# Keys and values of the first and last batch in 1 KB rows, and more transposes of batch 1 by DMA, in an attention-plus-FFN kernel

## The chip, the cores and the metric

The kernel runs on one core of a Trainium2 chip. A core has a matrix engine (TensorE, "PE" in the profile; its weight loads are "PEld"), a vector engine (VectorE, "DVE"), an activation engine (ScalarE, "ACT"), a general engine (GpSimd, "POOL") and a sync engine (SyncE, "SP") that here only issues DMA transfers. The engines run at the same time and wait for one another with semaphores. Matmuls write to PSUM[...]. The metric is the device time of one execution in microseconds (us), the median of several.

## What is computed

```python
# q, k, v: 8 batches, 8 heads, 576 positions, 64 wide, float32
theta = pi / 2 * pos / 576
phi(x) = concat([relu(x) * cos(theta), relu(x) * sin(theta)], axis=-1)   # 64 -> 128
kv  = einsum('bhsf,bhsd->bhfd', phi(k), v);   z = sum(phi(k), axis=s)
num = einsum('bhsf,bhfd->bhsd', phi(q), kv);  den = einsum('bhsf,bhf->bhs', phi(q), z) + 1e-6
x   = num / den                      # as 4608 tokens of 512 (heads side by side)
out = ((x @ w1) * (x @ w2)) @ w3 @ w_out   # 512 -> 1024 -> 1024 -> 512, float32
```

The sum over positions in `kv` does not depend on their order: keys and values may be spread over partitions in any way, as long as both are spread alike and each key row gets the cosine and sine of its own position. Queries are tied to the order of the tokens.

## The kernel before

Each batch's 576 positions are held as five chunks: chunks 0 to 3 with 128 positions (one per partition), chunk 4 with 64. There are two layouts. In the layout of the first and last batch ("own"), partition p holds positions 4p to 4p+3 in chunks 0 to 3, and chunk 4 is a transfer of its own, with rows of one position (64 float32, 256 bytes). In the layout of the other batches the first 64 partitions hold five positions each (rows of 1280 bytes) and the last 64 four each (1 KB):

```python
        at = src[b, :, 0:512, :].rearrange("h (p j) d -> p h j d", j=4)
        eng.dma_start(out=t[rows, :, c0:c0 + n, :].rearrange("p h j d -> p h (j d)"),
                      in_=at[rows, :, c0:c0 + n, :].rearrange("p h j d -> p h (j d)"))

    def load_first4(eng, t, src, b=0):
        eng.dma_start(out=t[0:64, :, 4, :], in_=src[b, :, 512:S, :].rearrange("h p d -> p h d"))

...
    def load(b, which, part=None):
        for name in which:
            src = {"k": k, "v": v, "q": q}[name]
            if part != 1:
                raw[b, name] = raw_tile(name)
            if b in own:
                half = slice(64 * part, 64 * part + 64)
                load_first(nc.gpsimd, raw[b, name], src, b=b, rows=half)
                if part == 1:
                    load_first4(nc.gpsimd, raw[b, name], src, b=b)
                continue
            if part != 1:
                nc.gpsimd.dma_start(
                    out=raw[b, name][0:64, :, :, :].rearrange("p h j d -> p h (j d)"),
                    in_=src[b, :, 0:320, :].rearrange("h (p j) d -> p h (j d)", j=5))
            if part != 0:
                nc.gpsimd.dma_start(
                    out=raw[b, name][64:128, :, 0:4, :].rearrange("p h j d -> p h (j d)"),
                    in_=src[b, :, 320:S, :].rearrange("h (p j) d -> p h (j d)", j=4))
```

Loads from GpSimd turn float32 into bf16 on the way. The keys of batch 0 come as float32 through SyncE. The start of the program:

```python
    k0 = raw[0, "k"] = wst.tile([P, H, NCH, D], FP32, name="kf", bufs=1)
    q0 = raw[0, "q"] = raw_tile("q")
    v0 = raw[0, "v"] = raw_tile("v")
    load_first(nc.sync, k0, k)
    load_first4(nc.sync, k0, k)
    load_first(nc.gpsimd, v0, v)
...
    idle_mms(27)                      # matmuls on zeros, while nothing has landed
    cosv, sinv = _trig_tables(nc, const)   # iotas on GpSimd, the rest on VectorE
    identb = const.tile([P, P], BF16, name="identb")
    load_first4(nc.gpsimd, v0, v)
    load_first(nc.gpsimd, q0, q, 0, 2)
    make_identity(nc, identb[:])
    load_first(nc.gpsimd, q0, q, 2, 2)
    load_w12(0, 256)
    load_w12(256, 256)
    load_first4(nc.gpsimd, q0, q)
    nc.gpsimd.dma_start(out=w1b[:, :, ds(512, 256)], in_=w1v[:, :, ds(512, 256)])

    def other_loads(behind):          # called once x chunk 0 of batch 0 is there
...
        for jp in range(8):
            load_w3(jp)
            if jp == 4:
                load(1, "k")
        load(1, "qv")
```

Features: `phi` of a chunk, its cosine half on VectorE (line 265) and its sine half on ScalarE (line 269). The column `at` of the tables follows the layout. A query chunk is then transposed, by PE and an evacuation of PSUM, or by a DMA transpose that SyncE issues:

```python
    def dma_q(b):
        return order_of(b)[5 if b == 0 else 2 if b == 1 else 0:]   # batch 1's order: 4, 0, 1, 2, 3

    def features(b, dst, src, c, cos=True, sin=True, scalar_heads=H):
        R = ROWS[c]
        at = c if b in own else NCH + c
...                                   # dst[:R, c] <- phi(src[:R, :, c]) with cosv[:R, at], sinv[:R, at]
    def prep_q(b, c):
        features(b, feat_of(b)[1], raw[b, "q"], c)
        if c in dma_q(b):
            R = ROWS[c]
            nc.sync.dma_start_transpose(out=att_of(b)["qpT"][:, :, ds(columns_of(b, c), R)],
                                        in_=feat[b][1][:R, c].rearrange("p h f -> p (h f)"))
```

`num` multiplies a transposed query chunk with `kvs` (the key-value sums) and normalises it into an x chunk; `x_tr` transposes that chunk into `xT`, from which the FFN reads tiles of 512 tokens:

```python
    def num(b, c, chain=True):
...
        def normalize():
            den = sm.tile([P, 2, 4], FP32, name="den")
            nc.vector.tensor_scalar_add(out=den[rows], in0=n4[:, :, :, 64], scalar1=1e-6)
            nc.vector.reciprocal(out=den[rows], in_=den[rows])
            nc.vector.tensor_tensor(out=xblk[rows], in0=n4[:, :, :, 0:D],
                                    in1=den[rows].unsqueeze(3).to_broadcast([R, 2, 4, D]),
                                    op=ALU.mult)

        if chain:
            normalize()
...
    def x_tr(b, c, by_vector=False, pst=None):
...
        if b >= 2:
            nc.sync.dma_start_transpose(out=xT[t][:, :, ds(o, R)], in_=xf)
            return
        if pst is None:
            pst = ps_tr.tile([P, 8, 128], BF16, name="pst")
        for kc in range(4):
            nc.tensor.transpose(pst[:, kc, 0:R], xf[:, ts(kc, 128)], identb[rows, rows])
        copy = nc.vector.tensor_copy if by_vector else nc.scalar.copy
        copy(out=xT[t][:, :, ds(o, R)], in_=pst[:, 0:4, 0:R])
```

The FFN runs tile by tile on PE (w1 and w2 products at line 464, the product with `w34b` at line 510). The other work is put in between by a table of slots: a slot is a place between two groups of FFN matmuls of a tile. Batch 0's first chunks come ahead of tile 0; batch 1 is worked through in slots 6 to 27 of tiles 0 and 1, while PE also multiplies w3 by w_out (line 232):

```python
            spread(prep_units(1, (prep_k,)), 6, 8, between)
            spread(prep_units(1, (prep_q,)), 10, 12, between)
            spread(prep_units(1, (prep_v,)), 13, 13, between)
            attention_at(1, between, kv=(14, 14, 14, 14, 14), tr=(12, 13, 17, 18, 19),
                         nu=(15, 17, 19, 20, 25), xt=(20, 20, 21, 22, 27))
            later = between[24:32]
            for i in range(2):
                between[11 + i].append(lambda i=i: behind_q(1, 2 + 2 * i, 2, "k", i))
            for i, g in enumerate((15, 17, 17, 19)):
                between[g].append(lambda i=i: behind_x(1, (i + 1) // 2, 2, "vvqq"[i], i % 2))
            for jp in range(8):
...                               # w3_tr, w34_mm, between
```

`behind_q(b, i, ...)` and `behind_x(b, i, ...)` make GpSimd wait for a query or x chunk before it issues the load named after it. The start of batch 0, in program order:

```python
    for c in range(NCH):
        prep_k(0, c)
    for c in range(NCH):
        prep_v(0, c)
    kv_steps = kv_first()
    next(kv_steps)
    q0f = feat[0][1]
    features(0, q0f, q0, 0, scalar_heads=4)
    next(kv_steps)
    prep_q(0, 1)
    idle_mms(2)
    q_tr_halves(0, 0)
    prep_q(0, 2)
    idle_mms(1)
    num(0, 0)
    q_tr(0, 1, evac=False)[1]()
    other_loads(att[0]["x"][0][:, 0, 0, 0:1])
    features(0, q0f, q0, 3, sin=False)
    q_tr(0, 2, evac=False)[1]()
    features(0, q0f, q0, 3, cos=False)
    idle_mms(1)
    x_tr(0, 0, by_vector=True,
         pst=unread[:, :].bitcast(BF16).rearrange("p (a b) -> p a b", b=128))
    num(0, 1)
```

Of the kernel before, what the change touches and what calls it, by code (L numbers as in the profile page):

```python
# [19 lines left out]
NCH = 5  # L20
# [48 lines left out]
def kernel(  # L69
# [48 lines left out]
    def raw_tile(name):  # L118
        return ld.tile([P, H, NCH, D], BF16, name=name + "s", bufs=2 if name == "k" else 1)

    def load(b, which, part=None):
        for name in which:
            src = {"k": k, "v": v, "q": q}[name]
            if part != 1:
                raw[b, name] = raw_tile(name)
            if b in own:
                half = slice(64 * part, 64 * part + 64)
                load_first(nc.gpsimd, raw[b, name], src, b=b, rows=half)
                if part == 1:
                    load_first4(nc.gpsimd, raw[b, name], src, b=b)  # L130
                continue
            if part != 1:
                nc.gpsimd.dma_start(
                    out=raw[b, name][0:64, :, :, :].rearrange("p h j d -> p h (j d)"),
                    in_=src[b, :, 0:320, :].rearrange("h (p j) d -> p h (j d)", j=5))
            if part != 0:
                nc.gpsimd.dma_start(
                    out=raw[b, name][64:128, :, 0:4, :].rearrange("p h j d -> p h (j d)"),
                    in_=src[b, :, 320:S, :].rearrange("h (p j) d -> p h (j d)", j=4))

# [13 lines left out]
    v0 = raw[0, "v"] = raw_tile("v")  # L154
    load_first(nc.sync, k0, k)
    load_first4(nc.sync, k0, k)
    load_first(nc.gpsimd, v0, v)
    zeros = const.tile([P, 512], BF16, name="zeros")
# [25 lines left out]

    idle_mms(27)
    cosv, sinv = _trig_tables(nc, const)
    identb = const.tile([P, P], BF16, name="identb")
    load_first4(nc.gpsimd, v0, v)
    load_first(nc.gpsimd, q0, q, 0, 2)
# [11 lines left out]
    def other_loads(behind):  # L201

        seen = sm.tile([P, 1], BF16, name="seen", bufs=1)
        nc.gpsimd.tensor_copy(out=seen[:], in_=behind)
        nc.gpsimd.dma_start(out=w2b[:, :, ds(512, 256)], in_=w2v[:, :, ds(512, 256)])
        load_w12(768, 256)
        nc.gpsimd.dma_start(out=woutb[:], in_=moe_w_out.rearrange("(c p) m -> p c m", p=P))
        for jp in range(8):
            load_w3(jp)
            if jp == 4:  # L210
                load(1, "k")
        load(1, "qv")


# [27 lines left out]
    def dma_q(b):  # L242

        return order_of(b)[5 if b == 0 else 2 if b == 1 else 0:]

# [13 lines left out]

    def features(b, dst, src, c, cos=True, sin=True, scalar_heads=H):  # L260

        R = ROWS[c]
        at = c if b in own else NCH + c
        if cos:
# [11 lines left out]
    def prep_k(b, c):  # L276
        features(b, feat_of(b)[0], raw[b, "k"], c)

    def prep_q(b, c):
        features(b, feat_of(b)[1], raw[b, "q"], c)  # L280
        if c in dma_q(b):
            R = ROWS[c]
            nc.sync.dma_start_transpose(out=att_of(b)["qpT"][:, :, ds(columns_of(b, c), R)],
                                        in_=feat[b][1][:R, c].rearrange("p h f -> p (h f)"))
# [60 lines left out]
    def num(b, c, chain=True):  # L345
# [15 lines left out]
        def normalize():  # L361
            den = sm.tile([P, 2, 4], FP32, name="den")
            nc.vector.tensor_scalar_add(out=den[rows], in0=n4[:, :, :, 64], scalar1=1e-6)  # L363
            nc.vector.reciprocal(out=den[rows], in_=den[rows])
            nc.vector.tensor_tensor(out=xblk[rows], in0=n4[:, :, :, 0:D],  # L365
                                    in1=den[rows].unsqueeze(3).to_broadcast([R, 2, 4, D]),
                                    op=ALU.mult)

# [6 lines left out]
    def x_tr(b, c, by_vector=False, pst=None):  # L375
        R, rows = ROWS[c], out_rows(b, c)
        xblk = att[b]["x"].pop(c)
        xf = xblk[rows].rearrange("p g h d -> p (g h d)")
# [5 lines left out]
        if t not in xT:  # L384
            xT[t] = xtp.tile([P, 4, 512], BF16, name="xT")
        if b >= 2:
            nc.sync.dma_start_transpose(out=xT[t][:, :, ds(o, R)], in_=xf)
            return
        if pst is None:
            pst = ps_tr.tile([P, 8, 128], BF16, name="pst")  # L390
        for kc in range(4):
            nc.tensor.transpose(pst[:, kc, 0:R], xf[:, ts(kc, 128)], identb[rows, rows])  # L392
        copy = nc.vector.tensor_copy if by_vector else nc.scalar.copy
        copy(out=xT[t][:, :, ds(o, R)], in_=pst[:, 0:4, 0:R])  # L394

# [196 lines left out]
    q0f = feat[0][1]  # L592
    features(0, q0f, q0, 0, scalar_heads=4)
    next(kv_steps)
# [7 lines left out]
    other_loads(att[0]["x"][0][:, 0, 0, 0:1])  # L602
    features(0, q0f, q0, 3, sin=False)
    q_tr(0, 2, evac=False)[1]()
    features(0, q0f, q0, 3, cos=False)
    idle_mms(1)
# [15 lines left out]
    for t in range(NT):  # L622
        slots = [[] for _ in range(24)]
        if t == 0:
# [16 lines left out]
            attention_at(1, between, kv=(14, 14, 14, 14, 14), tr=(12, 13, 17, 18, 19),  # L641
                         nu=(15, 17, 19, 20, 25), xt=(20, 20, 21, 22, 27))
            later = between[24:32]
            for i in range(2):
                between[11 + i].append(lambda i=i: behind_q(1, 2 + 2 * i, 2, "k", i))
            for i, g in enumerate((15, 17, 17, 19)):
# [48 lines left out]
```

## Time and profile before

| | |
|---|---|
| time, median of 3 runs | 249.24 us (249.07 to 249.59) |
| span of the profiled execution | 247.4 us |
| granted TensorE clock | 1.000 |
| read from HBM, written | 38.80 MB, 9.44 MB |
| share of 16 DMA engines: loads and stores from GpSimd; SyncE's queue | 72.7%; 33.4% |
| query transposes by DMA, x transposes by DMA | 33, 30 |
| mean time of an x copy out of PSUM, 128x512, ScalarE; VectorE | 0.59 us; 0.42 us |
| first FFN matmul | at 15.85 us |

The profile is of one execution. Its page has the busy time of each engine, the span in 40 slices with the busy share of each in tenths, the DMA queues, and the chain of work that ended last, followed back from the end: at each step to what released the instruction, or to the instruction before it on the same engine. A share of an engine in that chain is time that the result waited for it. Other views are the timeline (start, length, engine, line of the kernel, operation, output<-input, count, and in brackets the idle time before it and what ended it) and the list of waits. Line numbers in views are those of the kernel whose profile it is. Matmuls overlap, so that what one costs is read from the distance of the starts and not from its length. The trace also has the start, size and queue of each DMA packet; a packet is named by the bytes that it reads or writes, and a load that turns float32 into bf16 writes half of what it reads.

### The profile page before, as it was taken

How to read it: one execution, taken by the hardware profiler on the slowest of the kernel's cores; microseconds unless marked ns; L12 is line 12 of the kernel's file. 1: busy time of each engine (PE TensorE's matmuls, PEld its weight loads, DVE VectorE, ACT ScalarE, POOL GpSimd, SP SyncE). 2: the span in 40 equal slices, each digit the busy share in tenths (PEclk: the TensorE clock that was granted, in tenths of full speed). 3: DMA queues.
4: the chain of work that ended last, by engine and by line, in shares of the span. 5: the costliest groups of instructions: out<-in, count | busy, mean ns of one | idle time of the engine just before them, and what ended most of it. 6: DMA issues, size and time to landing. Idle time of an engine off the chain costs nothing.

```text
span 247.4 us, 4896 instructions
## 1 busy us (share of the span) xinstructions
PE 239.9 (97%) x1808; PEld 127.5 (52%) x1839; DVE 141.9 (57%) x333; ACT 123.2 (50%) x209; POOL 94.3 (38%) x189
## 2 busy tenths in 40 slices
PE   8899999999999999999999999999999999999994
PEld 2478555565554445544544455455545554444443
DVE  7776674656657555748465966566586555312421
ACT  2676325927852594267426832783287332323331
POOL 7755241215512442154113621562143008878100
PEclk9999999999999999999999999999999999999999
DMA  6999999999999999999989899999985938999413
GB/s 195 179 193 199 210 204 205 144 160 190 181 119 194 138 154 133 149 158 174 124 134 151 112 153 153 153 181 146 141 108 150 185 82 170 305 300 303 154 41 130
DMA packets 86087, 41.15 MB, mean 166 GB/s; under 512 B 53552, under 2 KB 82608, under 8 KB 86064
## 3 DMA queue, kind: packets, MB, share of 16 engines
q0 software_dynamic: 37072, 27.20, 72.7%
q1 hardware_dynamic: 48560, 13.18, 33.4%
q10 hardware_dynamic: 432, 0.46, 0.5%
q8 instruction: 14, 0.23, 0.4%
q14 instruction: 9, 0.07, 0.1%
HBM read 38.80 MB, written 9.44 MB: 195 GB/s over the span
## 4 chain that ended last, share of the span: by engine, by line
PE 92%; DMA 3%; issue 1%; DVE 1%; POOL 1%; ACT 0%; POOLq 0%
PE ffnps L464 50%; PE ffnps L510 24%; PE ffnps L232 5%; PE pnum L355 4%; PE pnum L297 4%; DMA qs<-in_q_dram 3%; PE pst L220 2%; PE pst L392 1%; PE pst L328 1%; PE ffnps L527 1%; POOL vs L112 0%; DVE xblk L365 0%; PE pfirst L355 0%; ACT xT L394 0%; DVE xT L394 0%
## 5 line engine op out<-in xcount | busy, mean ns | idle before, releaser
L505 DVE TENSOR_TENSOR abT<-asb,ffnps 128x512 bf16<-128x512 bf16 x68 | 46.6, 685 | 56.1 <-PE ffnps L464 55.9
L464 PE MATMUL ffnps<-xT,w1b 128*128 128x512 bf16 (+2 forms) x310 | 74.4, 357 | 0.9 <-ACT xT L394 0.2
L464 PE MATMUL ffnps<-xT,w2b 128*128 128x512 bf16 (+2 forms) x312 | 74.0, 357 | 0.4
L510 PE MATMUL ffnps<-w34b,abT 128*128 128x512 bf16 x271 | 64.7, 379 | 0.4
L501 ACT CAST asb<-ffnps 128x512 bf16<-128x512 f32 x68 | 39.8, 585 | 49.8 <-PE ffnps L464 48.4
L516 ACT COPY held<-ffnps 128x512 f32<-128x512 f32 x35 | 20.5, 586 | 49.6 <-PE ffnps L510 43.6
L464 PEld LDWEIGHTS <-w1b 128*128 128x128 bf16 x320 | 28.9, 98 | 27.7 <-issue 0.6
L464 PEld LDWEIGHTS <-w2b 128*128 128x128 bf16 x320 | 28.7, 98 | 26.9
L510 PEld LDWEIGHTS <-abT 128*128 128x128 bf16 x280 | 25.6, 98 | 26.4
L269 ACT ACTIVATE qp<-qs,sinv 128x512 bf16<-128x512 bf16 (+2 forms) x40 | 28.3, 715 | 2.1 <-DMA qs<-in_q_dram 2.0
L365 DVE TENSOR_TENSOR xblk<-pnum,den 128x512 bf16<-128x512 f32 (+1 forms) x39 | 26.9, 691 | 2.2
L269 ACT ACTIVATE kp<-ks,sinv 128x512 bf16<-128x512 bf16 (+1 forms) x35 | 24.5, 720 | 0.0
L438 POOL DMA_DIRECT2D out_dram<-held x42 | 22.1, 532 | 4.6 <-DMA out_dram<-held 1.8
L540 POOL COPY seen<-xblk 64x1 bf16<-64x1 bf16 x15 | 2.7, 183 | 53.4 <-DVE xblk L365 53.4
L355 PEld LDWEIGHTS <-qpT 128*128 128x128 bf16 x320 | 15.0, 98 | 10.2 <-issue 2.7
L540 POOL COPY seen<-qp 64x1 bf16<-64x1 bf16 x14 | 2.6, 183 | 40.6 <-DVE qp L265 40.6
L265 DVE TENSOR_SCALAR qp<-qs,cosv 128x512 bf16<-128x512 bf16 (+1 forms) x40 | 17.2, 434 | 1.2 <-DMA qs<-in_q_dram 1.2
L363 DVE TENSOR_SCALAR den<-pnum 128x8 f32<-128x8 f32 (+1 forms) x39 | 6.4, 164 | 19.4 <-PE pnum L355 19.4
L289 POOL COPY va<-vs 128x512 bf16<-128x512 bf16 (+1 forms) x30 | 17.5, 632 | 0.0
L297 PEld LDWEIGHTS <-kp 128*128 128x128 bf16 x280 | 13.0, 98 | 7.3
L355 PE MATMUL pnum<-kvs,qpT 128*128 128x65 bf16 x312 | 16.4, 194 | 0.2
L232 PE MATMUL ffnps<-woutb,w3T 128*128 128x512 bf16 x61 | 15.0, 379 | 0.1
(87 smaller groups left out, 184.2 us busy)
## 6 DMA issues: line engine op xcount, KB each, us to landing
out_dram<-held POOLq DMA_DIRECT2D x16, 256.0 KB, 4.6
out_dram<-held POOLq DMA_DIRECT2D x24, 128.0 KB, 3.9
qs<-in_q_dram POOLq DMA_DIRECT2D x10, 256.0 KB, 5.6
w3b<-in_moe_w_dram POOLq DMA_DIRECT2D x8, 256.0 KB, 13.4
ks<-in_k_dram POOLq DMA_DIRECT2D x8, 256.0 KB, 6.0
vs<-in_v_dram POOLq DMA_DIRECT2D x8, 256.0 KB, 6.4
ks<-in_k_dram POOLq DMA_DIRECT2D x6, 320.0 KB, 5.5
qs<-in_q_dram POOLq DMA_DIRECT2D x6, 320.0 KB, 5.3
```

Source lines behind the costliest of these rows:

```text
L232: nc.tensor.matmul(acc[:, :], lhsT=w3T[:, lc, :], rhs=woutb[:, lc, :], start=(lc == 0), stop=(lc == 7))
L269: nc.scalar.activation(out=dst[:R, c, 0:n, D:F], in_=src[:R, 0:n, c, :], func=ACTF.Relu, scale=sinv[:R, at:at + 1], bias=0.0)
L289: eng.tensor_copy(out=feat_of(b)[2][:R, c, :, 0:D], in_=raw[b, "v"][:R, :, c, :])
L297: nc.tensor.matmul(kvt[:, h // 4, ds((h % 4) * 65, 65)], lhsT=kp[:, c, h, :], rhs=va[:, c, h, 0:D + 1], start=(i == 0 and h % 4 == 0), sto ...
L355: nc.tensor.matmul(nt[:, h // 4, ds((h % 4) * 65, 65)], lhsT=qpT[:, h, ds(at, 128)], rhs=kvs[:, h, :], start=True, stop=True)
L365: nc.vector.tensor_tensor(out=xblk[rows], in0=n4[:, :, :, 0:D], in1=den[rows].unsqueeze(3).to_broadcast([R, 2, 4, D]), op=ALU.mult)
L438: eng.dma_start(out=rows[:, :, cols], in_=osb[64 * i:64 * i + rows.shape[0], :, cols])
L464: nc.tensor.matmul(out, lhsT=w[:, kc, ts(jc, 128)], rhs=x[:, kc, tok], start=(kc == 0), stop=(kc == 3))
L501: nc.scalar.copy(out=asb[:], in_=aT[:, :])
L505: nc.vector.tensor_mul(out=abT[:, jc, :], in0=asb[:], in1=bT[:, :])
L510: nc.tensor.matmul(ops[:, :], lhsT=abT[:, jc, ts(ms, 128)], rhs=w34b[:, jc, :], start=(jc == 0), stop=(jc == 7))
L516: nc.scalar.copy(out=osb[:, ms % 2, :], in_=ops[:, :])
```

## The change

Keys and values of batch 0 and of batch 7 take the layout of the other batches, so that no transfer with 256-byte rows is left for them; their queries keep their own. For this `features` is given the column of the tables by its caller. With it, one more query chunk of batch 1 (four of five) and two of its x chunks (3 and 4) are transposed by DMA instead of PE; the first half of batch 2's keys is loaded right behind batch 1's loads, and its second half behind the features of the first query chunk; there are 24 idle matmuls at the start in place of 27; the normalisation of x chunk 0 of batch 0 and the copies of x chunks 0 and 3 are cut in two, so that their steps overlap.

```diff
--- before.py
+++ after.py
@@ -118,25 +118,27 @@
     def raw_tile(name):
         return ld.tile([P, H, NCH, D], BF16, name=name + "s", bufs=2 if name == "k" else 1)
 
+    def load_half(eng, t, src, b, part):
+        if part == 0:
+            eng.dma_start(out=t[0:64, :, :, :].rearrange("p h j d -> p h (j d)"),
+                          in_=src[b, :, 0:320, :].rearrange("h (p j) d -> p h (j d)", j=5))
+        else:
+            eng.dma_start(out=t[64:128, :, 0:4, :].rearrange("p h j d -> p h (j d)"),
+                          in_=src[b, :, 320:S, :].rearrange("h (p j) d -> p h (j d)", j=4))
+
     def load(b, which, part=None):
         for name in which:
             src = {"k": k, "v": v, "q": q}[name]
             if part != 1:
                 raw[b, name] = raw_tile(name)
-            if b in own:
-                half = slice(64 * part, 64 * part + 64)
-                load_first(nc.gpsimd, raw[b, name], src, b=b, rows=half)
-                if part == 1:
-                    load_first4(nc.gpsimd, raw[b, name], src, b=b)
-                continue
-            if part != 1:
-                nc.gpsimd.dma_start(
-                    out=raw[b, name][0:64, :, :, :].rearrange("p h j d -> p h (j d)"),
-                    in_=src[b, :, 0:320, :].rearrange("h (p j) d -> p h (j d)", j=5))
-            if part != 0:
-                nc.gpsimd.dma_start(
-                    out=raw[b, name][64:128, :, 0:4, :].rearrange("p h j d -> p h (j d)"),
-                    in_=src[b, :, 320:S, :].rearrange("h (p j) d -> p h (j d)", j=4))
+            for i in (0, 1) if part is None else (part,):
+                if name == "q" and b in own:
+                    half = slice(64 * i, 64 * i + 64)
+                    load_first(nc.gpsimd, raw[b, name], src, b=b, rows=half)
+                    if i == 1:
+                        load_first4(nc.gpsimd, raw[b, name], src, b=b)
+                else:
+                    load_half(nc.gpsimd, raw[b, name], src, b, i)
 
     woutb = wst.tile([P, 8, DM], BF16, name="woutb", bufs=1)
     w3b = wst.tile([P, 8, DFF], BF16, name="w3b", bufs=1)
@@ -152,9 +154,9 @@
     k0 = raw[0, "k"] = wst.tile([P, H, NCH, D], FP32, name="kf", bufs=1)
     q0 = raw[0, "q"] = raw_tile("q")
     v0 = raw[0, "v"] = raw_tile("v")
-    load_first(nc.sync, k0, k)
-    load_first4(nc.sync, k0, k)
-    load_first(nc.gpsimd, v0, v)
+    for half in range(2):
+        load_half(nc.sync, k0, k, 0, half)
+    load_half(nc.gpsimd, v0, v, 0, 0)
     zeros = const.tile([P, 512], BF16, name="zeros")
     nc.vector.memset(zeros[:], 0.0)
     va_bufs, kp_bufs, qp_bufs = [], [], []
@@ -182,10 +184,10 @@
         for _ in range(n):
             nc.tensor.matmul(unread[:, :], lhsT=zeros[:, 0:128], rhs=zeros[:], start=True, stop=True)
 
-    idle_mms(27)
+    idle_mms(24)
     cosv, sinv = _trig_tables(nc, const)
     identb = const.tile([P, P], BF16, name="identb")
-    load_first4(nc.gpsimd, v0, v)
+    load_half(nc.gpsimd, v0, v, 0, 1)
     load_first(nc.gpsimd, q0, q, 0, 2)
     make_identity(nc, identb[:])
     load_first(nc.gpsimd, q0, q, 2, 2)
@@ -210,6 +212,7 @@
             if jp == 4:
                 load(1, "k")
         load(1, "qv")
+        load(2, "k", 0)
 
 
     w3Ts = {}
@@ -241,7 +244,7 @@
 
     def dma_q(b):
 
-        return order_of(b)[5 if b == 0 else 2 if b == 1 else 0:]
+        return order_of(b)[5 if b == 0 else 1 if b == 1 else 0:]
 
     feat = {}
 
@@ -257,10 +260,9 @@
             att[b] = {"qpT": phi.tile([P, H, S], BF16, name="qpT"), "x": {}}
         return att[b]
 
-    def features(b, dst, src, c, cos=True, sin=True, scalar_heads=H):
+    def features(dst, src, c, at, cos=True, sin=True, scalar_heads=H):
 
         R = ROWS[c]
-        at = c if b in own else NCH + c
         if cos:
             nc.vector.tensor_scalar(out=dst[:R, c, :, 0:D], in0=src[:R, :, c, :], scalar1=0.0,
                                     scalar2=cosv[:R, at:at + 1], op0=ALU.max, op1=ALU.mult)
@@ -274,10 +276,10 @@
                                         op0=ALU.max, op1=ALU.mult)
 
     def prep_k(b, c):
-        features(b, feat_of(b)[0], raw[b, "k"], c)
+        features(feat_of(b)[0], raw[b, "k"], c, NCH + c)
 
     def prep_q(b, c):
-        features(b, feat_of(b)[1], raw[b, "q"], c)
+        features(feat_of(b)[1], raw[b, "q"], c, c if b in own else NCH + c)
         if c in dma_q(b):
             R = ROWS[c]
             nc.sync.dma_start_transpose(out=att_of(b)["qpT"][:, :, ds(columns_of(b, c), R)],
@@ -362,9 +364,12 @@
             den = sm.tile([P, 2, 4], FP32, name="den")
             nc.vector.tensor_scalar_add(out=den[rows], in0=n4[:, :, :, 64], scalar1=1e-6)
             nc.vector.reciprocal(out=den[rows], in_=den[rows])
-            nc.vector.tensor_tensor(out=xblk[rows], in0=n4[:, :, :, 0:D],
-                                    in1=den[rows].unsqueeze(3).to_broadcast([R, 2, 4, D]),
-                                    op=ALU.mult)
+            n = 1 if b == 0 and c == 0 else 2
+            for i in range(2 // n):
+                g = ts(i, n)
+                nc.vector.tensor_tensor(out=xblk[rows, g], in0=n4[:, g, :, 0:D],
+                                        in1=den[rows, g].unsqueeze(3).to_broadcast([R, n, 4, D]),
+                                        op=ALU.mult)
 
         if chain:
             normalize()
@@ -374,7 +379,7 @@
 
     def x_tr(b, c, by_vector=False, pst=None):
         R, rows = ROWS[c], out_rows(b, c)
-        xblk = att[b]["x"].pop(c)
+        xblk = att[b]["x"][c]
         xf = xblk[rows].rearrange("p g h d -> p (g h d)")
         if b % 2 == 0:
             slot = S * b + 128 * c
@@ -383,15 +388,19 @@
         t, o = divmod(slot, 512)
         if t not in xT:
             xT[t] = xtp.tile([P, 4, 512], BF16, name="xT")
-        if b >= 2:
+        if b >= 2 or b == 1 and c >= 3:
             nc.sync.dma_start_transpose(out=xT[t][:, :, ds(o, R)], in_=xf)
             return
         if pst is None:
             pst = ps_tr.tile([P, 8, 128], BF16, name="pst")
-        for kc in range(4):
-            nc.tensor.transpose(pst[:, kc, 0:R], xf[:, ts(kc, 128)], identb[rows, rows])
-        copy = nc.vector.tensor_copy if by_vector else nc.scalar.copy
-        copy(out=xT[t][:, :, ds(o, R)], in_=pst[:, 0:4, 0:R])
+        copies = [nc.vector.tensor_copy if by_vector else nc.scalar.copy] * 2
+        if b == 0 and c == 3:
+            copies[1] = nc.vector.tensor_copy
+        n = 2 if b == 0 and c in (0, 3) else 4
+        for i in range(4 // n):
+            for kc in range(n * i, n * i + n):
+                nc.tensor.transpose(pst[:, kc, 0:R], xf[:, ts(kc, 128)], identb[rows, rows])
+            copies[i](out=xT[t][:, ts(i, n), ds(o, R)], in_=pst[:, ts(i, n), 0:R])
 
     def attention_at(b, slots, kv, tr, nu, xt):
 
@@ -590,7 +599,7 @@
     kv_steps = kv_first()
     next(kv_steps)
     q0f = feat[0][1]
-    features(0, q0f, q0, 0, scalar_heads=4)
+    features(q0f, q0, 0, 0, scalar_heads=4)
     next(kv_steps)
     prep_q(0, 1)
     idle_mms(2)
@@ -600,9 +609,9 @@
     num(0, 0)
     q_tr(0, 1, evac=False)[1]()
     other_loads(att[0]["x"][0][:, 0, 0, 0:1])
-    features(0, q0f, q0, 3, sin=False)
+    features(q0f, q0, 3, 3, sin=False)
     q_tr(0, 2, evac=False)[1]()
-    features(0, q0f, q0, 3, cos=False)
+    features(q0f, q0, 3, 3, cos=False)
     idle_mms(1)
     x_tr(0, 0, by_vector=True,
          pst=unread[:, :].bitcast(BF16).rearrange("p (a b) -> p a b", b=128))
@@ -639,10 +648,9 @@
             spread(prep_units(1, (prep_q,)), 10, 12, between)
             spread(prep_units(1, (prep_v,)), 13, 13, between)
             attention_at(1, between, kv=(14, 14, 14, 14, 14), tr=(12, 13, 17, 18, 19),
-                         nu=(15, 17, 19, 20, 25), xt=(20, 20, 21, 22, 27))
+                         nu=(15, 17, 19, 20, 25), xt=(15, 20, 21, 22, 25))
             later = between[24:32]
-            for i in range(2):
-                between[11 + i].append(lambda i=i: behind_q(1, 2 + 2 * i, 2, "k", i))
+            between[10].append(lambda: behind_q(1, 0, 2, "k", 1))
             for i, g in enumerate((15, 17, 17, 19)):
                 between[g].append(lambda i=i: behind_x(1, (i + 1) // 2, 2, "vvqq"[i], i % 2))
             for jp in range(8):
```

## The prediction

> **What bounds the kernel now.** I read the page first: busy shares, the row of slices, the chain that ended last.
>
> ```profile
> PE 239.9 (97%) x1808; PEld 127.5 (52%) x1839; DVE 141.9 (57%) x333; ACT 123.2 (50%) x209; POOL 94.3 (38%) x189
> ...
> PE   8899999999999999999999999999999999999994
> ...
> PE 92%; DMA 3%; issue 1%; DVE 1%; POOL 1%; ACT 0%; POOLq 0%
> ```
>
> TensorE (PE) works in every slice, and 92% of the chain is matmuls. The rest sits at the front: one DMA wait of 3%. So there are two ways to gain: let the stream of real matmuls begin earlier, or take work out of it. What VectorE, ScalarE and GpSimd save counts only if one of those two follows. The chain over the first 26 us (start, length, what) shows what sets the beginning:
>
> ```profile
> 1.28 1.04 POOL vs L112
> ...
> 3.56 8.02 DMA qs<-in_q_dram
> ...
> 12.60 0.44 DVE qpT L342
> ...
> 14.19 0.70 DVE xblk L365
> ...
> 14.93 0.41 PE unread L392 x4
> ...
> 15.37 0.44 DVE xT L394
> ...
> 15.85 1.05 PE ffnps L464 x16
> ...
> 21.85 0.59 ACT xT L394
> ```
>
> The first FFN matmul runs at 15.85 us. It waits for x chunk 0 of batch 0, that for the first query chunk, which lands at 11.58 (3.56 + 8.02). The keys and values are only just ahead of the query, as the timeline shows (start, length, engine, line, operation):
>
> ```profile
> 6.84 3.17 ACT L269 ACTIVATE kp<-kf,sinv 128x512 bf16<-128x512 f32 x5 [4.61 <-DMA kf<-in_k_dram]
> 9.68 1.25 DVE L289 COPY va<-vs 128x512 bf16<-128x512 bf16 x5 [0.59 <-DMA vs<-in_v_dram]
> 10.03 0.29 PE L314 MATMUL kva<-va,kp 128*128 128x65 bf16 x4 [0.59 <-ACT kp L269]
> ```
>
> Values land at 9.68, their copies run to 10.93, and the key-value matmuls keep pace from 10.03 to about 11.4. From 15.85 on PE hardly waits; the largest wait, some 0.2 us before 22.49, is for the ScalarE copy of x chunk 3 (21.85). Last, I read the PE timeline around batch 1 for the price of the transposes:
>
> ```profile
> 49.17 0.61 PE L328 MATMUL pst<-identb,qp 128*128 128x128 bf16 x8
> 49.61 1.03 PE L232 MATMUL ffnps<-woutb,w3T 128*128 128x512 bf16 x4
> ...
> 57.88 0.62 PE L392 MATMUL pst<-identb,xblk 64*128 64x64 bf16 x8
> 58.40 0.42 PE L355 MATMUL pnum<-kvs,qpT 128*128 128x65 bf16 x8
> ...
> 65.47 0.40 PE L392 MATMUL pst<-identb,xblk 128*128 128x128 bf16 x4
> 65.71 1.03 PE L464 MATMUL ffnps<-xT,w1b 128*128 128x512 bf16 x3
> ```
>
> Because matmuls are pipelined, the price is from one start to the next: 0.44 us for the eight of a query chunk, 0.24 for the four of x chunk 3, and 0.52 for those of x chunks 4 and 0 together, so about 0.28 for chunk 4.
>
> [...] counted by their starts, the packets of values that read 1 KB go at 97 per 0.25 us (397 GB/s read), those that read 256 bytes at 137 (140 GB/s). [...] keys run alone to about 5 us, and values, issued at 1.28, have no packet before 5.5. [...] the weight loads of the idle matmuls are 0.43 us apart until 5.4, and the last fifteen take 3.12 us (0.21 each). So three idle matmuls fewer end the warm-up at about 8.8 instead of 9.44[...].
>
> **The change part by part.** *Start.* Keys and values of batch 0 lose a set of 512 packets of 256 bytes each; the bytes move into 512 rows of 1280 and 512 of 1024. By the rates above, 512 small packets of values take 512/137 x 0.25 = 0.93 us; the same 131 KB at 395 GB/s take 0.33. Saving 0.6. For keys the small packets go at up to 157 per 0.25 us: 0.82 us, against 0.34 at the 385 GB/s of their large ones. Saving 0.48. Both sets lie ahead of the first query packets, and the DMA engines are never idle there, so the query should land about 1.05 us earlier, near 10.5. Before, the main part of a tensor landed without its small rows; now chunks 0 to 3 need both halves. Keys: first part at 6.75 before, all of it 0.3 later now, near 7.05. Values: they begin after the keys; 0.48 saved on keys, 0.33 more bytes of their own to wait for, so 9.4 to 9.5 instead of 9.68. GpSimd also issues half as many descriptors in the first values load (an issue of 512 rows takes 0.70 us at lines 133 and 137, against 1.04), which puts the later issues 0.35 earlier; I count nothing for it, since the data are what is late.
>
> Then the chain: ScalarE's key features end 0.3 later, near 10.3, still ahead of the fifth chunk's matmuls; key-value matmuls end near 11.1 (before about 11.4); the query features start when VectorE is through with the value copies, 10.65, instead of 11.6; PE comes to the query transposes near 11.45 instead of 12.16, after the two idle matmuls that stand there. The start therefore moves by 0.7, not by 1.05: the value copies and key-value matmuls take over as the last wait. Splitting the first normalisation and the first x copy in two lets half 0 be transposed while half 1 is multiplied. Little comes of it, as VectorE is busy with a query feature (0.34) in between: 0.1. Sum at the start: 0.8.
>
> *Chunk 3 of batch 0.* Its x copy is split over ScalarE and VectorE, which takes most of the wait at 22.1 to 22.5: 0.2.
>
> *Batch 1.* One query chunk and two x chunks go from PE to DMA transposes: 0.44 + 0.28 + 0.24 = 0.96 out of the stream. One VectorE copy of 0.42 and two ScalarE copies (0.4 and 0.59) go too, which is off the path.
>
> *Loads after it.* The first half of batch 2's keys is issued without a gate; its second half is gated earlier. It is behind batch 1's values in the same queue, and takes data traffic out of the time in which the query transposes run.
>
> *Last batch.* Two sets of 256-byte rows fewer near 180 us, where PE is full and loads have slack: 0.
>
> What gives some back: batch 1's values are DMA-bound. Their copies begin at 48.84 and end at 50.24, and PE uses them at 50.48. They move by the 1.05 us of DMA saved plus the 0.2 of slack; PE would come 0.8 + 0.2 + 0.44 = 1.44 earlier. Stall 0.2. Sum: 0.8 + 0.2 + 0.96 - 0.2 = 1.76; I take 1.65, since the split copies and the transposes' landing are the less certain terms. 249.24 - 1.65 = 247.6 us.
>
> **The rivals.** *Transposes that land late.* Before, the three query transposes of batch 1, issued at 48.16, 49.6 and 52.25, land 6.3 to 8.0 us later (packets from 51.0 to 57.9), and the chunks are used at 56.67, 58.40 and 63.42. With four of them, an x chunk behind them and the use 1.3 us earlier, the second or third could come 0.5 to 1.5 late, and x chunk 4 (wanted at about 60.1, when tile 1 starts) as well. For it: one issue keeps SyncE's queue 1.3 to 2.5 us. Against it: the first issue moves from 48.16 to about 46.5, because the chunk that was done on PE now leads, and batch 2's keys, which ran in the midst of the transposes at 52 to 54, are mostly gone by then. It would make 248.3 to 249.3. *The start does not move*, because values land no earlier or keys' features become the bound: only the 1.0 to 1.2 of batch 1 and chunk 3 is left, 248.2. *The start moves by the whole 1.05 and Pool's 0.35 as well*: that three idle matmuls (0.65 us) were taken out fits values that come clearly earlier. It would be 247.0. *PE cools down in the longer gap*: [...] I see nothing for it.
>
> **Range and chances.** Everything the change can reach is in the first 66 us and within 2.2 us of gain. 247.6 is the middle; the good rival gives 246.8 with the stall gone, the bad one 248.8. Two per cent are 5 us, three times the gain, so "within 2%" is nearly certain; a stall of 5 us would need a transfer that nothing here points to.
>
> **What would show it.** Right: the query lands near 10.5 and the first FFN matmul comes near 15.05; values near 9.5, keys near 7.05; no PE transposes but one query chunk in batch 1; the FFN of tile 1 at about 60.0 instead of 61.70; from there to the end the same distance as now. Wrong: a wait of PE on a transposed query or on x between 50 and 62; a first FFN matmul after 15.5; key-value matmuls at half clock.

## The result, and the profile after

The changed kernel takes 255.5 us (254.7 to 255.84) against 249.23 before: a ratio of 1.0245, interval 1.0219 to 1.0271, or 6.1 us more by that ratio. The prediction was 247.6 us with a range of 246.8 to 248.8. The span of the profiled execution is 253.9 us against 247.4.

The page of the changed kernel, the lines that answer to those shown of before, and the row of the granted clock:

```profile
PE 240.3 (95%) x1789; PEld 127.7 (50%) x1820; DVE 140.7 (55%) x335; ACT 122.1 (48%) x207; POOL 92.4 (36%) x186
...
PE   8488999998999999999999999999999999999994
...
PEclk9979999999999999999999999999999999999998
...
PE 83%; DMA 10%; DVE 3%; issue 1%; ACT 1%; SPq 0%; DVEq 0%
```

PE is busy for as long as before. The span has grown by time in which PE waits: the second and third slices (6 to 19 us) have a hole, and the clock falls in the third (by the trace it is halved from 13.6 to 17.0 us). DMA is now 10% of the chain instead of 3%. Of that, 9.2 us are the keys at the start. Another 17.3 us are two query transposes under way (6.8 us from 51.40, 10.5 from 172.71); PE does other work during most of them and waits 1.5 us for them in all. The chain over the first 26 us (start, length, what):

```profile
0.74 0.75 SPq L123
...
1.54 9.21 DMA kf<-in_k_dram
...
13.30 0.29 PE kva L316 x4
...
18.45 0.76 DVE xblk L370 x2
...
19.72 0.28 PE unread L402 x2
20.01 0.02 issue
20.03 0.29 DVE xT L403
```

The wait for the query (8.02 us before) has given way to one for the keys: `kf` is complete at 10.75 us, where its main part was there at 6.75. The timeline shows what follows from it:

```profile
10.86 2.20 DVE L267 TENSOR_SCALAR kp<-kf,cosv 128x512 bf16<-128x512 f32 x5 [4.85 <-DMA kf<-in_k_dram]
10.87 3.17 ACT L271 ACTIVATE kp<-kf,sinv 128x512 bf16<-128x512 f32 x5 [8.63 <-DMA kf<-in_k_dram]
...
12.98 1.08 DVE L291 COPY va<-vs 128x512 bf16<-128x512 bf16 x5
...
13.30 0.29 PE L316 MATMUL kva<-va,kp 128*128 128x65 bf16 x4 [4.00 <-DVE va L291]
...
20.38 0.38 PE L473 MATMUL ffnps<-xT,w1b 128*128 128x128 bf16 x4
```

The first FFN matmul runs at 20.38 us instead of 15.85, 4.53 later. The values are no longer what is waited for: their copies (12.98) stand in VectorE's queue behind the key features. The list of PE's waits shows the rest:

```profile
PE kva L316 <- DVE va L291: 4.0, 1, 4.0
PE pnum L357 <- DMA qpT<-qp: 1.5, 2, 1.1
...
PE unread L402 <- DVE xT L403: 0.5, 1, 0.5
PE pst L402 <- ACT xT L403: 0.5, 1, 0.5
```

1.1 us is the first DMA-transposed query of batch 1 (at 58.25), 0.4 a query of batch 7 (at 183.29); the two waits of 0.5 stand in the middle of the split x copies. Laying the ScalarE copies of FFN products of both traces side by side gives the lag of the changed kernel along the way: 4.84 us in tile 0, 5.8 after the first queries of batch 1, 5.26 in tile 1, 5.6 at 110 us, 6.2 near 180, and 6.5 in the span. So 1.2 us of it arise behind tile 1. Each profile is of one execution, and some tenths of such a lag can be chance: in e12 below, which changes only loads of the last batch, it is 0.30 in tile 0 and 0.66 from tile 1 on.

### The profile page after: what moved, and what is told of

The parts are those of the page before. It is cut to its first block, busy times and chain, and to the rows that moved or that the text cites. A ratio compares the mean times of both kernels' runs of the same rounds, so it can differ in the third digit from the quotient of the medians.

```text
span 253.9 us, 4864 instructions
## 1 busy us (share of the span) xinstructions
PE 240.3 (95%) x1789; PEld 127.7 (50%) x1820; DVE 140.7 (55%) x335; ACT 122.1 (48%) x207; POOL 92.4 (36%) x186
## 4 chain that ended last, share of the span: by engine, by line
PE 83%; DMA 10%; DVE 3%; issue 1%; ACT 1%; SPq 0%; DVEq 0%
PE ffnps L473 47%; PE ffnps L519 21%; DMA qpT<-qp 7%; PE pnum L357 4%; PE ffnps L235 4%; DMA kf<-in_k_dram 4%; PE pnum L299 3%; PE pst L223 1%; DVE xblk L370 1%; DVE kp L267 1%; PE ffnps L536 1%; PE pst L402 1%; ACT kp L271 1%; PE kva L316 0%; PE pnum L316 0%
## 5 line engine op out<-in xcount | busy, mean ns | idle before, releaser
L525 ACT COPY held<-ffnps 128x512 f32<-128x512 f32 x35 | 20.5, 586 | 51.7 <-PE ffnps L519 48.5
L291 POOL COPY va<-vs 128x512 bf16<-128x512 bf16 (+1 forms) x30 | 17.5, 632 | 0.2 <-DMA vs<-in_v_dram 0.2
```

Of the source, the lines that this page charges most:

```text
L525: nc.scalar.copy(out=osb[:, ms % 2, :], in_=ops[:, :])
```

## Experiments

The theory after this reading: three parts of the change cost time, each by itself. The largest is the load of the float32 keys in two halves of 64 partitions. First, each part alone, on top of the kernel before; then the mechanism of the two larger ones. Ratios are to the kernel before, run on the same chip.

**e1, the start alone.**

```diff
-    load_first(nc.sync, k0, k)
-    load_first4(nc.sync, k0, k)
-    load_first(nc.gpsimd, v0, v)
+    for half in range(2):
+        load_half(nc.sync, k0, k, 0, half)
+    load_half(nc.gpsimd, v0, v, 0, 0)
...
-    idle_mms(27)
+    idle_mms(24)
...
-    load_first4(nc.gpsimd, v0, v)
+    load_half(nc.gpsimd, v0, v, 0, 1)
```

> The kernel before with the new key and value loads of batch 0 and 24 idle matmuls, nothing else. Theory A ([...] the first half of the float32 keys runs at 205 GB/s and its second half shares the engines with the values): keys land near 10.8 as in the changed kernel, the first FFN matmul comes near 20.2, time 253.5 to 254.2, a ratio of 1.017 to 1.020. Rival B (the late keys are a chance of that one profile, or come from the other changes): keys near 7.1, time 248.5 to 249.

253.93 us, ratio 1.0177 (1.0160 to 1.0194): +4.4 us. Keys land at 10.76, the first FFN matmul runs at 20.33. Theory A; from the timeline:

```profile
10.86 2.20 DVE L266 TENSOR_SCALAR kp<-kf,cosv 128x512 bf16<-128x512 f32 x5 [4.87 <-DMA kf<-in_k_dram]
...
20.33 0.38 PE L470 MATMUL ffnps<-xT,w1b 128*128 128x128 bf16 x4 [0.15 <-DVE xT L400]
```

**e2, batch 1 alone** (`dma_q` from the second chunk on, x chunks 3 and 4 by DMA, `load(2, "k", 0)` without a gate, `behind_q(1, 0, 2, "k", 1)` in slot 10).

> The kernel before with the changes of batch 1 alone: four query chunks and x chunks 3 and 4 by DMA transposes, first half of batch 2's keys ungated. Theory A (these transposes land late by their own doing: four in a row, each taking SyncE 1.3 to 3 us): PE waits about 1.1 to 1.3 us for the first transposed query, which eats the 0.96 us of PE work taken out: 249.2 to 249.9. Rival B (they were late only because everything was late): no wait over 0.2 us, 248.2 to 248.6.

250.18 us, ratio 1.0038 (1.0023 to 1.0053): +0.9 us, above both ranges, though on the side of A. The wait is there with a start that is not late; from the PE timeline:

```profile
53.52 0.43 PE L357 MATMUL pnum<-kvs,qpT 128*128 128x65 bf16 x8 [1.13 <-DMA qpT<-qp]
...
59.23 0.42 PE L357 MATMUL pnum<-kvs,qpT 128*128 128x65 bf16 x8 [0.23 <-DVE xblk L370]
...
62.52 1.03 PE L471 MATMUL ffnps<-xT,w1b 128*128 128x512 bf16 x4
```

Tile 1 begins at 62.52, 0.8 later than before, although PE has less to do. The second wait, 0.23 for a normalisation, is one that the x transposes on PE used to cover. Further on in tile 1 the lag of this profile is 0.53 us; it rises to 1.10 at 110.31, where PE has a wait of 0.41 that ends with key features of ScalarE (`kp`). The changed kernel has such a wait of 0.18 at 114.80. In e4, which has the same changes of batch 1, the lag stays at 0.99 from 87 us to the end, so these later waits may be chance. Nor is the 1.1 us the same in every execution (e4).

**e3, the splits alone** (the `n` and `copies` lines of `normalize` and `x_tr`).

> The kernel before with the split normalisation and the split x copies of chunks 0 and 3 alone. Theory A (the second half's transposes wait for the first half's copy, since both halves are in one PSUM tile: 0.5 us twice in the changed kernel): the first FFN matmul at 16.1 to 16.3 instead of 15.85 and a wait of 0.5 at chunk 3: 249.5 to 250.0. Rival B (the halves overlap as meant): 248.9 to 249.2.

249.85 us, ratio 1.0015 (1.0005 to 1.0025): +0.4 us. Theory A; the timeline around the first copy:

```profile
14.74 0.28 PE L401 MATMUL unread<-identb,xblk 128*128 128x128 bf16 x2
...
15.20 0.28 DVE L402 COPY xT<-unread 128x256 bf16<-128x256 bf16 x1
...
15.53 0.27 PE L401 MATMUL unread<-identb,xblk 128*128 128x128 bf16 x2 [0.50 <-DVE xT L402]
...
16.19 0.38 PE L472 MATMUL ffnps<-xT,w1b 128*128 128x128 bf16 x4
```

The second pair of transposes has its data at 15.02 (both normalisations, 14.26 + 0.76) and starts at 15.53, when the copy of the first pair has ended. Both pairs write one PSUM tile, and the wait ends with the copy that reads that tile (VectorE reads PSUM here, as `xT<-unread` shows); so the program orders the write behind the read. (Halves in two tiles were not tried.) Two halves in sequence take longer than one whole: FFN at 16.19 instead of 15.85. At chunk 3 the same wait is 0.46.

**e4, all but the start** (the changed kernel with the removed lines of e1 put back).

> The changed kernel with batch 0's keys and values as before and 27 idle matmuls. If the parts add up, it is e2 plus e3 minus the time before, plus the loads of the last batch, which should be 0 to 0.4 (one wait of 0.41 for a query of batch 7 in the changed kernel): 249.3 to 250.5 by theory A of both. If the start is the whole of the loss (rival): 247.9 to 248.3.

251.17 us, ratio 1.0074 (1.0053 to 1.0095). The time is above both ranges. The ratios of e2, e3 and e12 (below, 0.0009) add up to 0.0062, which is inside the interval. With e1 the four parts make 0.0239 of the 0.0245: within the intervals the parts add, and no loss from their meeting is measured. The profile of this run shows how much the late query varies: with the same changes of batch 1 as in e2, and batch 2's keys again issued next to the first transpose (47.65 and 47.66), PE waits only 0.24 us for it (at 53.67), and the lag behind the kernel before shrinks by 0.4 us from 32 to 69 us; 0.30 of that is lost again at 75.03, for a query of batch 2. The ten times of this run go from 249.96 to 253.78. So the 1.1 us of e2 and of the changed kernel is what two profiles show and no constant of the change.

**e5, both halves of the keys at once.**

```diff
-    for half in range(2):
-        load_half(nc.sync, k0, k, 0, half)
+    for half, eng in enumerate((nc.sync, nc.scalar)):
+        load_half(eng, k0, k, 0, half)
```

> e1 (the new loads of batch 0 alone) with the two halves of the keys issued at once, one by SyncE and one by ScalarE. Theory A ([...] the two streams do not take from each other): about 380 GB/s together, last key packet near 5.8, keys land near 6.8, values as in e1 or sooner, time 248.4 to 249.4. Rival B (two transfers share the DMA engines and only take turns): as slow together as one after the other, keys near 9 to 10.8, 252.5 to 254.

253.79 us, ratio 1.0163 (1.0130 to 1.0197): rival B. The keys are complete at 9.97:

```profile
9.97 2.06 DVE L266 TENSOR_SCALAR kp<-kf,cosv 128x512 bf16<-128x512 f32 x5 [3.98 <-DMA kf<-in_k_dram]
```

Both halves are issued at 0.7 us. By the packets of the trace ScalarE's half ran alone until 4.46, with 86 to 90 packets of 1 KB per 0.25 us from 3.25 to 3.75 and with 46 to 48 (190 to 197 GB/s) after 4.0. SyncE's had its first packet then and its last at 8.5 (36 to 41 of 1280 bytes per 0.25 us from 6 to 7.75, 184 to 210 GB/s). From 4.5 to 5.25 both were under way, and together moved 186 to 193 GB/s. Why they went almost one after the other, and were no faster while both ran, is not shown.

**e6, PE kept busy** (`idle_mms(46)` in e1).

> e1 with 46 idle matmuls instead of 24, so that PE works until about 12.7 us and keeps its clock. Theory A (of the 4.5 us of late start about 1 is the halved clock in 10 to 17.5 us): granted clock 1.0 throughout, key-value matmuls 0.13 us a group of four instead of 0.22, first FFN matmul at 19.2 to 19.6 instead of 20.33, time 252.8 to 253.3. Rival B (the start follows the landing of the query and keys only): no change, 253.8 to 254.

Busy times and granted clock by stretch (us; then PE, PEld, DVE, ACT, POOL busy, clock, DMA share, GB/s), first of e1:

```profile
12.50:15.00 2.50, 1.69 (x32) 1.69 (x32) 2.28 (x10) 1.94 (x4) 0.33 (x1) 0.50 1.57 192
15.00:17.50 2.50, 2.50 (x24) 1.69 (x22) 0.52 (x2) 1.88 (x4) 0.00 (x0) 0.50 1.45 195
```

and of e6:

```profile
12.50:15.00 2.50, 2.50 (x48) 1.82 (x46) 2.24 (x9) 1.82 (x4) 0.29 (x1) 1.00 1.59 191
15.00:17.50 2.50, 2.39 (x37) 1.70 (x34) 1.50 (x6) 1.99 (x5) 0.00 (x0) 1.00 1.45 196
```

The clock stays whole, and the first FFN matmul runs at 19.04 instead of 20.33, as theory A has it or better. The time does not follow, and is that of B: 253.94 us, ratio 1.0176 (1.0139 to 1.0213), against 1.0177 (1.0160 to 1.0194) of e1. By these intervals a gain of up to about 1 us could be hidden (an estimate: 0.004 of 249 us), a whole 1.3 hardly. In the two profiles the span is 251.6 against 252.1, so 0.8 of the 1.3 us is given back on the way; all of it goes near 160 us, where PE waits 0.66 us for a ScalarE copy in e6 and not in e1. Whether that wait is chance is not known. The halved clock is a cost in the trace that is not found in the time, and this is left open.

**e7, the values after the keys** (e1 with the values' loads behind a GpSimd copy that waits for the second half of the keys).

> e1 with the values issued only when all keys have landed, so that the keys have the DMA engines to themselves. Its time says nothing (later values, 254 to 258); its packets do. Theory A ([...] whatever the row): the second half's 1 KB rows run alone at about 200 GB/s (50 packets per 0.25 us, 85 to 110 ns each) and end near 8.2. Rival B (rows of 1280 bytes are the slow ones): they run at 93 to 96 packets per 0.25 us, 46 ns each, as the 1 KB rows over 128 partitions did, and end near 6.9. Rival C (only the sharing with the values was slow): both halves near 380 GB/s, all keys out by 5.5.

The 1 KB rows of the second half, alone on the engines, ran at 51 to 54 packets per 0.25 us (209 to 221 GB/s), 82 to 88 ns each, from 6.25 to 7.25, and ended at 7.9. Theory A: it is not the length of the row. Nor is sharing with the values the only trouble: without any sharing the keys still take from 2.25 to 7.9. But each half starts faster than it goes on: the first has 75 packets per 0.25 us at 3.5 (384 GB/s) and 37 to 43 from 4.25 to 4.75, the second 61 and 71 from 5.75 to 6.25. Its time, 256.95 us in one run, is that of values that start late.

**e9, the five-position half across partition 64** (e7 with the first half in partitions 32 to 95, the second in 0 to 31 and 96 to 127, its values unmoved: the sums are then of mismatched positions; 255.19 us in one run).

> e7 (keys alone on the engines, values after them) with the five-position half of the keys put into partitions 32 to 95 in place of 0 to 63, and the four-position half into partitions 0 to 31 and then 96 to 127. The value rows stay where they were, so keys and values no longer match: the key-value sums are those of mismatched positions, and the time says nothing. What counts is the key packets. Theory A ([...]): the 1280-byte packets now run at 70 to 80 per 0.25 us (350 to 400 GB/s), 55 to 60 ns each, done by about 4.8; the two pieces of 32 partitions after them at 45 to 52 per 0.25 us (200 GB/s) each. Rival B (any transfer to 64 partitions is slow): 36 to 43 per 0.25 us and 110 to 120 ns, as in e7.

The packets of the keys in the four cases, counted in the traces by their start; this is no view of the profile:

```
keys (float32)                  partitions   window       packets  mean    written
before, 1 KB rows               0-127        4.00-4.25      95     47 ns   389 GB/s
changed, 1280-byte rows         0-63         3.50-3.75      78     55 ns   399 GB/s
changed, 1280-byte rows         0-63         4.50-4.75      35    119 ns   179 GB/s
changed, 1280-byte rows         0-63         5.00-5.25      39    119 ns   200 GB/s
e7, 1 KB rows alone             64-127       6.50-6.75      53     83 ns   217 GB/s
e9, 1280-byte rows              32-95        4.00-4.25      76     55 ns   389 GB/s
```

The same rows, the same 64 partitions in number, and once the load is under way twice the rate, only because the range crosses partition 64. Theory A for these packets, the last of which starts at 5.15, against 5.5 in e7 and 5.8 in the changed kernel. The half rate is no fixed speed of such a load, though: from 3.25 to 4.0 us the changed kernel's went at 292 to 399 GB/s (the second line has the middle of it), and only from 4.0 at 179 to 205. Why the first packets go faster is not shown. For the two pieces of 32 partitions the theory had 45 to 52 packets per 0.25 us; they began with 64 to 92 and then went at 52 to 70. (The last packet of each kind started at 5.7 before, for the 1 KB rows, and at 5.8 and 9.6 in the changed kernel for the first and the second half.)

Once a load into 64 partitions on one side of partition 64 is under way the runs agree: 179 to 221 GB/s. Near its start they do not: up to 399. Why such a load falls to that rate, and one across partition 64 does not, is not shown by these runs. Two queues at once brought nothing: e5 has 253.79 us against 253.93 of e1. Side by side two loads did run at 7.0 us in the changed kernel: keys to partitions 64 to 127 at 164 GB/s written and values to 0 to 63 at 92, together 256, more than either half took alone for long.

**e8, half of batch 2's keys later** (e2 with its second half behind x chunk 4).

> e2 (batch 1's changes alone) with the second half of batch 2's keys issued only behind x chunk 4 of batch 1. Theory A (the first query transposes are held up by the load that runs beside them): packets of the first transpose start 1.2 to 2 us after its issue, no wait of PE for a query over 0.2 us, 248.5 to 249.3 if the late keys cost nothing later. Rival B (a DMA transpose needs its 6 to 7 us here anyway): the wait of about 1.1 us stays, 250 or more.

250.26 us, ratio 1.0022 (1.0008 to 1.0037), which is not clear of e2's 1.0038. The wait for the first query is gone; the PE timeline:

```profile
52.24 0.42 PE L357 MATMUL pnum<-kvs,qpT 128*128 128x65 bf16 x8
...
57.94 0.42 PE L357 MATMUL pnum<-kvs,qpT 128*128 128x65 bf16 x8 [0.23 <-DVE xblk L370]
```

The first transpose, issued at 46.93, has its first packets at 48.5, 1.6 us later, where in e2 they started 2.7 us after the issue at 46.83 and ran among the keys' until 52. So A holds for the wait, and B for the total: the key half now comes too late for ScalarE. The chain of this run:

```profile
54.39 4.75 DMA ks<-in_k_dram
59.23 0.72 ACT kp L271
...
62.05 1.89 PE ffnps L471 x8
```

On ScalarE the late key features (0.72 us from 59.23, 0.62 from 60.42) stand ahead of x copies, the last of which runs from 61.51 to 62.01, and tile 1 begins at 62.05.

**e10, only x chunks 3 and 4 by DMA** (with the x slots of the changed kernel).

> The kernel before with only x chunks 3 and 4 of batch 1 by DMA transposes (query chunks as before). Theory A (x transposes land with slack: chunk 4 is there long before tile 1 wants it): 0.52 us of PE work out of the stream and no new wait, 248.6 to 248.9. Rival B (num of the third chunk then waits 0.23 us for the second's normalisation, as in e2, and the next transposes come later): 249.0 to 249.3.

249.33 us, ratio 0.9991 (0.9978 to 1.0004): closest to B, no difference that is measured. The PE timeline shows the 0.28 of chunk 4 turned into a wait:

```profile
57.85 0.39 PE L392 MATMUL pst<-identb,xblk 128*128 128x128 bf16 x4
58.46 0.42 PE L355 MATMUL pnum<-kvs,qpT 128*128 128x65 bf16 x8 [0.23 <-DVE xblk L365]
```

With eight transposes in that place PE came to `num` when the normalisation before it had ended (58.40 in the kernel before); with four it comes earlier and waits until 58.46. Only the 0.24 of chunk 3 is left, seen as a lead of 0.25 at 66.6 us.

**e11, e2 with batch 2's keys gated as before.**

> e2 (batch 1's changes alone) with both halves of batch 2's keys gated as in the kernel before. Theory A (the wait of 1.1 us for the first transposed query comes from the load that runs beside it; gated later, it starts only after the first transpose has been issued): the wait shrinks to 0 to 0.5, 248.3 to 249.0. Rival B (with the second half gated behind the third and fifth query chunk the loads fall into the same time and the wait stays): 249.8 to 250.3.

252.51 us, ratio 1.0111 (1.0086 to 1.0137): both theories missed, it is worse. The PE timeline:

```profile
53.58 0.43 PE L356 MATMUL pnum<-kvs,qpT 128*128 128x65 bf16 x8 [1.57 <-DMA qpT<-qp]
...
59.40 0.43 PE L356 MATMUL pnum<-kvs,qpT 128*128 128x65 bf16 x8 [1.68 <-DMA qpT<-qp]
```

The load that was issued between the transposes ran ahead of the later ones: from 50.5 to 52 the trace has 424 packets of keys and 18 of transposes. Moving batch 2's keys forward was right, then: by the ratios of e11 and e2 (1.0111 and 1.0038) it saved some 1.8 us of what four transposes would otherwise have cost here. (Both halves move between the two runs.)

**e12, the last batch alone** (batch 7's keys and values in the new rows).

> The kernel before with the new key and value loads of the last batch alone. Theory A: no effect, PE is full there, 249.0 to 249.7 (ratio 0.998 to 1.002). Rival B (the wait of 0.41 us for a query of batch 7 in the changed kernel comes from these loads): 249.7 to 250.0 and such a wait near 177 to 183 us.

249.43 us, ratio 1.0009 (0.9995 to 1.0022). Theory A: no effect that is measured. The longest wait for a transposed query is 0.18, at 57.32, so the 0.41 at batch 7 in the changed kernel does not come from these loads alone.

## Why the prediction was wrong

*What bounds the kernel* was read rightly: a PE stream without gaps behind a front that waits for transfers. Four parts make 0.0239 of the 0.0245, and each of them is in the prediction. "From there to the end the same distance as now" failed in the profile, whose lag grows by 1.2 us behind tile 1, with PE waits of 0.18 and 0.41 there; as e4 has no such growth, this may be chance.

*The start* is the step that failed: "Saving 0.48" for the keys, and with it "keys ... near 7.05" and "the start therefore moves by 0.7". I gave the moved bytes the rate of the large packets seen, 385 GB/s. That rate was measured on rows to all 128 partitions. The new halves go to 64 partitions each and run at about 200: in e7, where nothing else is moving, the keys need 2.25 to 7.9 us, 5.6 us, where 1.18 MB at 385 GB/s would be 3.1 us (an estimate from that rate). The kernel before could not show it: its loads of 64 partitions turn float32 into bf16, and write half of what they read. At 35.5 us it has 150 packets of 640 bytes in half a microsecond, 192 GB/s written and 384 read: such a load reads at nearly the full rate while it writes at that of the halves here. Only the float32 keys, which have the same row length on both sides, would have to write faster. Then the second half, still unsent when the values begin, shares with them (40 packets of keys beside 36 of values per 0.25 us at 7.0 us), which is why they end later in the changed kernel than in e7. So of the 3.7 us by which the keys miss 7.05, 1.7 are the sharing (9.6 against 7.9) and the rest comes with the half rate. Measured: +4.4 us (e1) where -0.7 was predicted, without the splits.

*The values' share*, 0.33 more bytes against 0.93 of small packets, was never reached as a bound: the keys hid it. Whether it would save 0.6 was not tried alone, since keys and values must have one layout.

*The splits*: "0.1" and "0.2" gained, +0.4 measured (e3). I counted what VectorE does in between, and not that the two halves share a PSUM tile, where the second write waited 0.5 us for the first read.

*Batch 1*: the price list of 0.96 us holds as work: from the first 512-wide FFN product to the key-value matmuls of batch 1 the distance is 24.91 us instead of 25.36, the 0.44 of one query chunk. But 0.28 of the rest became a wait for the normalisation (e10), and the query landed late. The rival "transposes that land late" named it with 0.5 to 1.5 us; 1.1 was seen in two profiles (0.24 in e4's), and for the first transposed chunk and not for "the second or third". I had put it aside because batch 2's keys would be "mostly gone by then". They were not: their second half was issued together with the first transpose (46.61 and 46.83 in e2). The part was to gain 0.76 (0.96 less a stall of 0.2) and lost 0.9 (e2): the term is off by 1.7 us. How much of that the late query makes on average is open, since the wait varies.

*The last batch*: 0, as said.

*The cooling PE*: "I see nothing for it" was wrong. PE had a gap of 4.0 us (waiting until 13.30), and the clock was at half from 13.6 to 17.0. In e6, where the idle matmuls last to 13.8 us and leave no such gap, it stays at 1.00 from 12.5 to 17.5, against 0.50 in e1; how long a gap it takes was not measured. What it cost in the time is open (e6).

*The range* was too narrow even by its own terms: "within 2.2 us of gain" leaves out its good rival, 246.8, which is 2.4 us. A loss was not in it at all, because no term had a load that gets slower.

## What to carry to other kernels

A rate taken from packets held here only for the partitions that they went to: before a transfer is cut into two of 64 partitions, work out what each writes per second. Here a half below or above partition 64 held about 200 GB/s and one across it 389; that the latter also brings the time back was not measured. PE work that is moved to DMA is gained only if no wait stood behind it (e10) and if the DMA lands in time; loads issued next to the transposes decided the latter here (PE waited 1.13 us for the first query in e2, not at all in e8, 1.57 in e11). Cutting a copy in two lost 0.4 us where both halves used one PSUM tile.

## What was not expected

Two queues with a 64-partition transfer each went almost one after the other (e5), and were no faster in the 0.75 us in which both ran. A load into one half, once it had got going, went at 292 to 399 GB/s for some 0.75 us before it fell to 179 to 205 (e9). A load of 320 KB issued amid transposes took the engines nearly alone for 1.5 us (e11). And 1.3 us of earlier FFN start (e6) did not show in the time: 1.0176 against 1.0177, each with an interval of 0.002 to 0.004.
